# Attention beside two dense layers: sums of a on TensorE, maxima of phi in three steps, later loads, four x buffers, v_m w_in over four turns

## The chip, the cores and the metric

The kernel runs on one core of a Trainium2 chip. The metric is device time in microseconds, from the first to the last work of one launch. The engines are TensorE (PE: matmuls, with its weight loads listed apart as PEld), VectorE (DVE), ScalarE (ACT), GpSimd (POOL) and SyncE (SP). Each works through its own instructions in program order, and in this kernel SP issues every DMA transfer.

## The reference

```python
# q, k, v: 8 batches x 8 heads x 576 x 64; phi: 8 x 8 x 576 x 32
a = phi - np.max(phi, axis=2, keepdims=True)          # over the 576 positions
a = np.exp(a)
a = a / (np.sum(a, axis=2, keepdims=True) + 1e-09)
k_m = np.einsum('bhsm,bhsd->bhmd', a, k)
v_m = np.einsum('bhsm,bhsd->bhmd', a, v)
scores = np.matmul(q, k_m.transpose(0, 1, 3, 2)) / np.sqrt(64)
attn = softmax(scores)                                 # over the 32 memories
x = np.matmul(attn, v_m)                               # to 4608 tokens x 512
h = x @ moe_w_in;  x = (h - np.tanh(h)) @ moe_w_out    # 512 -> 2048 -> 512
h = x @ moe2_w_in; g = np.where(h > 0, h, np.exp(np.minimum(h, 0)) - 1)
return g @ moe2_w_out
```

## The kernel before, in words

The program has three parts that overlap.

**Attention units.** A unit is one batch and four heads; there are 16 (u = 0 to 15). `Attention.unit` is a generator: each `yield` ends a step, and the program calls every live unit once in a round. A step emits instructions into the engines' queues, so the round in which something is emitted sets its place in the order of every engine. A unit takes, in this order: the maximum of phi over six chunks (L120, DVE), its maximum over partitions by a transpose and a matmul (L125 to L134), the subtraction (L135), the exponential into a (L140, ACT), the sum of a over six chunks (L143, DVE), the matmuls of a with k and v into km (L150) and the sums' column of km (L153), 1/sum (rs), rm, kk and vbd (L159 to L165), transposes of q (L174), scores (L195), the softmax over memories (L199 to L211) and the probabilities split in two parts, phl (L215, L216), stored in DRAM (L222). Units 0 and 2 run in one set of tiles, all others in another; units 0 and 1 do their elementwise work on DVE, the rest on POOL. Tiles of phi and of kv have one buffer, so the load for the next unit must wait until this unit's last reader is done. Units 4 and up start seven rounds apart, so up to three are alive.

**First layer, 64 blocks.** A block is 288 tokens by 512 of the 2048 hidden columns, in two turns (i = 0, 1). Attention is not multiplied out: v_m times w_in is formed first (`vw_half`, L316 to L321: six matmuls, two copies on ACT, two subtractions on DVE for both parities), and a block multiplies the probabilities p with it (`h_unit`, L331). `g_a` to `g_d` compute h - tanh(h): four ACT instructions (L342 to L345; the third writes s), then POOL (L350) and DVE (L351, L356, L357), and a split of s into g by ACT and POOL (L363, L364). `x_unit` multiplies an earlier block's g with w_out (L376) and copies the result to an x tile (L383 on ACT, L385 on DVE), which is stored in DRAM (L391). There are three x tiles, three s tiles, and three PSUM banks (`misc`) that the x matmuls, v_m w_in and the attention units share. A group is four blocks (j = 0 to 3) that share v_m w_in; in the last of them each turn computes two halves of it for the next group. The order of a turn is written out by hand: h_unit, g_a, g_b, an x_unit, a round of conversions of weights, a round of the units, g_d, half of v_m w_in, an x_unit, g_c, a round of the units, the other half.

**Second layer.** From about 945 us on PE multiplies the sums of x with the second pair of weights; its loads (`load_x`, L405) begin in the last blocks of the first layer.

## Time and profile before

| | |
|---|---|
| median of 3 runs | 1772.01 us (1768.45 to 1779.19) |
| the profiled execution | 1771.73 us |
| its span, first to last instruction | 1770.0 us |
| PE / DVE / ACT / POOL busy | 1618.5 / 1225.3 / 954.7 / 766.3 us |
| mean granted TensorE clock | 0.968 |

The profile is of one execution. Busy times are those in which an engine had an instruction running; a wait is the idle time of an engine ahead of an instruction, put down to what ended it. PEclk is the granted share of TensorE's full clock. "SPq" is the queue of SP, whose instructions issue transfers; its waits are times in which nothing behind them can be issued.

### The profile page before, as it was taken

The numbers are of one execution on the slowest core, as the hardware profiler recorded it, in microseconds if no ns is written. First come the engines' busy times: TensorE is split into PE (matmuls) and PEld (weight loads), VectorE is DVE, ScalarE is ACT, GpSimd is POOL, SyncE is SP. The second block draws the span as 40 slices with busy tenths as digits, with TensorE's granted clock in tenths as the row PEclk, the third lists the DMA queues.
The fourth block names the chain that finished last, engine by engine and source line by source line (L and its number), as shares of the span: only waits on it lengthen the run. The fifth ranks groups of instructions, "written<-read, shape, count | busy, mean of one in ns | idle before, by whom it ended". The sixth has DMA issues, their size and how long they took to land.

```text
span 1770.0 us, 30078 instructions
## 1 busy us (share of the span) xinstructions
PE 1618.5 (91%) x11496; PEld 1494.5 (84%) x11496; DVE 1225.3 (69%) x1805; ACT 954.7 (54%) x1713; POOL 766.3 (43%) x539
## 2 busy tenths in 40 slices
PE   4546887987998999999989999999999999999998
PEld 3446777877898999999989999999999999999997
DVE  5768876778899988888854555555555555555554
ACT  2445675766888888888864333333333333333332
POOL 2144554636676666666653222222222222222222
PEclk9668999999999999999999999999999999999999
DMA  9546557567566455666567521212222121111110
GB/s 226 157 121 181 146 158 201 169 191 221 187 225 195 160 177 212 217 215 223 189 191 291 195 61 60 60 60 60 60 60 59 54 58 56 57 60 57 58 36 25
DMA packets 140935, 238.40 MB, mean 135 GB/s; under 512 B 8184, under 2 KB 102392, under 8 KB 138744
## 3 DMA queue, kind: packets, MB, share of 16 engines
q1 hardware_dynamic: 140792, 236.49, 43.0%
q8 instruction: 91, 1.49, 0.4%
q14 instruction: 52, 0.43, 0.1%
HBM read 159.78 MB, written 75.50 MB: 133 GB/s over the span
## 4 chain that ended last, share of the span: by engine, by line
PE 70%; DMA 10%; DVE 7%; ACT 5%; issue 3%; POOL 2%; SPq 1%; DVEq 0%; POOLq 0%; ACTq 0%
PE h_ps L432 23%; PE o_ps L469 22%; PE x_ps L376 14%; PE h_ps L331 8%; DMA x_dram<-x 5%; DMA raw<-in_moe_w_in_dram 3%; PE vw_ps L316 2%; DVE s L356 1%; DVE vw L321 1%; DMA kv<-in_v_dram 1%; ACT t L342 1%; DMA xr<-x_dram 1%; DMA phi<-in_phi_dram 1%; ACT u L343 1%; ACT big L345 1%
## 5 line engine op out<-in xcount | busy, mean ns | idle before, releaser
L376 PE MATMUL x_ps<-g,w 128*128 128x288 f32 x3072 | 454.5, 301 | 30.4 <-DVE vw L321 9.6
L376 PEld LDWEIGHTS x_ps<-g,w 128*128 128x128 f32 x3072 | 427.2, 192 | 41.6 <-ACT x L383 11.0
L458 POOL TENSOR_TENSOR e<-hm,e 128x512 fp32r<-128x512 f32 x144 | 186.8, 1297 | 588.1 <-ACT e L457 435.4
L432 PEld LDWEIGHTS h_ps<-x,wi 128*128 128x128 f32 x3456 | 429.7, 190 | 11.7
L432 PE MATMUL h_ps<-x,wi 128*128 128x256 f32 x3456 | 433.2, 281 | 0.0
L469 PE MATMUL o_ps<-wo,e 128*128 128x512 f32 x1728 | 423.8, 394 | 0.7 <-POOL e L458 0.7
L469 PEld LDWEIGHTS o_ps<-wo,e 128*128 128x128 f32 x1728 | 314.8, 188 | 65.0 <-POOL e L458 1.1
L443 ACT ACTIVATE t_ps<-hm 128x512 f32<-128x512 f32 x144 | 86.7, 602 | 515.1 <-DVE hm L442 515.1
L350 POOL TENSOR_TENSOR v<-t,u 128x576 f32<-128x576 f32 x128 | 183.9, 1436 | 230.8 <-ACT u L343 208.4
L331 PE MATMUL h_ps<-p,vw 128*128 128x288 f32 x1536 | 241.8, 309 | 17.8 <-DVE s L357 6.1
L331 PEld LDWEIGHTS h_ps<-p,vw 128*128 128x128 f32 x1536 | 222.9, 199 | 20.9 <-issue 12.7
L364 POOL TENSOR_TENSOR g<-s,g 128x576 fp32r<-128x576 f32 x128 | 203.2, 1588 | 83.9 <-ACT g L363 81.3
L449 DVE SCALAR_TENSOR_TENSOR hm<-hm,t_ps 128x512 f32<-128x512 f32 x144 | 99.1, 688 | 200.6 <-ACT hm L444 200.6
L442 DVE TENSOR_SCALAR hm<-h_ps 128x512 f32<-128x512 f32 x144 | 99.6, 692 | 139.9 <-PE h_ps L432 139.9
L351 DVE TENSOR_TENSOR h_ps<-h_ps,t 128x576 f32<-128x576 f32 x128 | 97.9, 765 | 56.8 <-ACT u L343 55.6
L342 ACT ACTIVATE t<-h_ps 128x576 f32<-128x576 f32 x128 | 83.2, 650 | 82.2 <-PE h_ps L331 39.6
L356 DVE SCALAR_TENSOR_TENSOR s<-s,v 128x576 f32<-128x576 f32 x128 | 121.5, 949 | 1.8 <-POOL v L350 1.8
L321 DVE TENSOR_TENSOR vw<-vw_ps,vw 64x512 fp32r<-64x512 f32 x128 | 88.1, 688 | 40.4 <-ACT vw L319 38.4
L357 DVE COPY_PREDICATED s<-big,h_ps 128x576 f32<-128x576 uint32 x128 | 106.3, 831 | 11.3 <-DVE s L356 0.5
L345 ACT ACTIVATE big<-u,bias 128x576 f32<-128x576 f32 x128 | 97.5, 762 | 13.5 <-DVE s L357 13.5
L451 DVE TENSOR_TENSOR hm<-hm,h_ps 128x512 f32<-128x512 f32 x144 | 98.9, 687 | 5.0
L450 DVE SCALAR_TENSOR_TENSOR hm<-hm,t_ps 128x512 f32<-128x512 f32 x144 | 98.9, 687 | 4.9
(86 smaller groups left out, 1764.6 us busy)
## 6 DMA issues: line engine op xcount, KB each, us to landing
x_dram<-x SPq DMA_DIRECT2D x128, 288.0 KB
xr<-x_dram SPq DMA_DIRECT2D x72, 512.0 KB
p<-p_dram SPq DMA_DIRECT2D x62, 576.0 KB
raw<-in_moe_w_in_dram SPq DMA_DIRECT2D x32, 512.0 KB
raw<-in_moe_w_out_dram SPq DMA_DIRECT2D x32, 512.0 KB
w_dram<-wst SPq DMA_DIRECT2D x32, 512.0 KB
kv<-in_k_dram SPq DMA_DIRECT2D x16, 576.0 KB
kv<-in_v_dram SPq DMA_DIRECT2D x16, 576.0 KB
```

The costliest lines, as they stand in the source:

```text
L321: nc.vector.tensor_tensor(lo, src, r32(hi), op=ALU.subtract)
L331: nc.tensor.matmul(ps[:, j, :NB], lhsT=vw[a][:, kc, 128 * j:128 * j + 128], rhs=p[:, kc, b, :], start=(k == 0), stop=(k == 5))
L342: nc.scalar.activation(t, w[0], ACTF.Tanh)
L345: nc.scalar.activation(big, u, ACTF.Relu, bias=bias[:, 1:2])
L350: nc.gpsimd.tensor_tensor(v, t, u, op=ALU.mult)
L356: nc.vector.scalar_tensor_tensor(s, s, G_B, v, op0=ALU.add, op1=ALU.mult)
L357: nc.vector.copy_predicated(s, big.bitcast(U32), d)
L364: nc.gpsimd.tensor_tensor(g[:, 1], s, r32(g[:, 0]), op=ALU.subtract)
L376: nc.tensor.matmul(ps, lhsT=wo[pg][:, a, j, 128 * dm:128 * dm + 128], rhs=g[:, b, j, :], start=(k == 0), stop=(k == 11))
L432: nc.tensor.matmul(ps[:, j], lhsT=w3[:, a, kc, 128 * j:128 * j + 128], rhs=x[:, b, kc, :], start=(k == 0), stop=(k == 11))
L458: nc.gpsimd.tensor_tensor(e[:, 1], hm, r32(e[:, 0]), op=ALU.subtract)
L469: nc.tensor.matmul(self.acc[n][tg], lhsT=e[:, a, j, 128 * tg:128 * tg + 128], rhs=w4[:, b, j, :], start=(pg == 0 and j == 0 and i == 0), s ...
```

## The change

- The sum of a over chunks on DVE (L143) and its tile go, and so does the round that it had. In place of four matmuls of the sums with ones there are six, one for each chunk, with a (128 columns) as weights.
- The maximum of phi is taken in three two-input steps (384, 128 and 128 elements) in place of one reduction. The first uses the buffer of pT.
- vbd is made by two instructions with two scalars each; rm goes.
- The load of phi for units 2 and up is issued by ACT. The loads of kv and q come after a `yield`, so a round behind the instructions that free their tiles. For units 4 and up a `yield` is put ahead of the store of phl.
- x has four buffers, s (`gw`) two.
- From block 26 on the halves of v_m w_in for the next group are computed in the four turns of j = 2 and 3, one in each. A second pool holds the tiles of the odd parity for every other group.

```diff
@@ -82,8 +82,7 @@
         self.kv = fix.tile([128, 2, 4, 6, D], F32, name="kv")
         self.a = fix.tile([128, 6, 4, M], F32, name="a")
         self.kT = fix.tile([128, 4, 2, M], F32, name="kT")
-        self.asum = fix.tile([128, 4, M], F32, name="asum")
-        for t in (self.a, self.asum, self.kv):
+        for t in (self.a, self.kv):
             nc.gpsimd.memset(t[96:], 0.0)
         nc.gpsimd.memset(self.kT, 0.0)
 
@@ -99,7 +98,7 @@
             nc.sync.dma_start(out=t[:96, 1], in_=view("v", 0, 4))
         elif what == "phi":
             t = self.wk.tile([96, 4, 6, M], F32, tag="phi", name="phi")
-            nc.sync.dma_start(out=t, in_=view("phi", 0, 4))
+            (nc.sync if u < 2 else nc.scalar).dma_start(out=t, in_=view("phi", 0, 4))
         else:
             t = self.q_p.tile([96, 2, 6, D], F32, tag="q", name="q")
             nc.sync.dma_start(out=t, in_=view("q", 0 if what == "q0" else 2, 2))
@@ -111,13 +110,16 @@
         b, g = divmod(u, 2)
         par = b % 2
         ident = self.ident
-        kv, a, kT, asum = self.kv, self.a, self.kT, self.asum
+        kv, a, kT = self.kv, self.a, self.kT
         ps_tile = lambda shape, name: self.ps.tile(shape, F32, tag="m", name=name)
 
         ph = self.loaded.pop((u, "phi"))
         row = lambda name: wk.tile([128, 4, M], F32, tag="cmax", name=name)
         cmax = row("cmax")[:96]
-        nc.vector.tensor_reduce(cmax, ph.rearrange("p h c m -> p h m c"), axis=AX.X, op=ALU.max)
+        top = wk.tile([128, S], F32, tag="pT", name="top")[:96, :12 * M].rearrange("p (h c m) -> p h c m", h=4, c=3)
+        nc.vector.tensor_tensor(top, ph[:, :, 0:3], ph[:, :, 3:6], op=ALU.max)
+        nc.vector.tensor_tensor(cmax, top[:, :, 0], top[:, :, 1], op=ALU.max)
+        nc.vector.tensor_tensor(cmax, cmax, top[:, :, 2], op=ALU.max)
         yield
         if u >= 4:
             yield
@@ -140,8 +142,6 @@
         nc.scalar.activation(a[:96].rearrange("p c h m -> p h c m"), ph, ACTF.Exp)
         self.load(nxt, "phi")
         yield
-        nc.vector.tensor_reduce(asum[:96], a[:96].rearrange("p c h m -> p h m c"), axis=AX.X, op=ALU.add)
-        yield
         self.loaded.pop((u, "kv"))
         km = ps_tile([128, 2 * D + 2], "km")
         kmv = km[:, :2 * D].rearrange("p (t d) -> p t d", t=2)
@@ -149,21 +149,20 @@
             for h in range(4):
                 nc.tensor.matmul(kmv[32 * h:32 * h + 32], lhsT=a[:, c, h, :], rhs=kv[:, :, h, c, :],
                                  start=(c == 0), stop=(c == 5))
-        for h in range(4):
-            nc.tensor.matmul(km[32 * h:32 * h + 32, 2 * D:], lhsT=asum[:, h], rhs=self.ones[:, :2],
-                             start=True, stop=True)
-        self.load(nxt, "kv")
+        for c in range(6):
+            nc.tensor.matmul(km[:, 2 * D:], lhsT=a[:, c].rearrange("p h m -> p (h m)"), rhs=self.ones[:, :2],
+                             start=(c == 0), stop=(c == 5))
         rs = sm.tile([128, 1], F32, tag="rs", name="rs")
-        rm = sm.tile([128, 2, 1], F32, tag="rm", name="rm")
         twice = lambda t: kmv[:, t].rearrange("p (o d) -> p o d", o=1).to_broadcast([128, 2, D])
         nc.vector.tensor_scalar(rs, km[:, 2 * D:2 * D + 1], GUARD, None, op0=ALU.add)
         nc.vector.reciprocal(rs, rs)
-        nc.vector.tensor_scalar(rm[:, :, 0], self.pmask, rs, None, op0=ALU.mult)
         kk = wk.tile([128, 2, D], F32, tag="kk", name="kk")
         nc.vector.tensor_scalar(kk, twice(0), rs, None, op0=ALU.mult)
         vbd = wk.tile([128, 2, D], F32, tag="vbd", name="vbd")
-        nc.vector.tensor_tensor(vbd, twice(1), rm.to_broadcast([128, 2, D]), op=ALU.mult)
-        yield
+        for j in range(2):
+            nc.vector.tensor_scalar(vbd[:, j], kmv[:, 1], rs, self.pmask[:, j:j + 1], op0=ALU.mult, op1=ALU.mult)
+        yield
+        self.load(nxt, "kv")
         s = self.sc_p.tile([128, 18, M], F32, tag="s", name="s")
         for pr in range(2):
             qt = self.loaded.pop((u, f"q{pr}"))
@@ -174,9 +173,9 @@
                     nc.tensor.transpose(pq[:, c2, :], qt[:, h, 2 * c2:2 * c2 + 2, :].rearrange("p c d -> p (c d)"),
                                         ident[:96, :96])
                 nc.scalar.activation(qT[:, h], pq, ACTF.Copy)
+                yield
                 if h == 1:
                     self.load(nxt, f"q{pr}")
-                yield
             if pr == 0:
                 kT_ps = ps_tile([128, 2, 128], "kT_ps")
                 nc.tensor.transpose(kT_ps[:, 0, :], kk.rearrange("p h d -> p (h d)"), ident)
@@ -215,6 +214,8 @@
         nc.scalar.activation(phl[:, :, 0], pTv, ACTF.Copy)
         eng.tensor_tensor(phl[:, :, 1], pTv, r32(phl[:, :, 0]), op=ALU.subtract)
         yield
+        if u >= 4:
+            yield
         for c, t in enumerate(first_p or ()):
             for hq in range(2):
                 r0 = 64 * hq + 32 * c
@@ -287,11 +288,12 @@
         self.tc, self.nc, self.const = tc, tc.nc, const
         self.p_dram, self.x2_dram = p_dram, x2_dram
         pool = lambda name, n, **kw: ctx.enter_context(tc.tile_pool(name=name, bufs=n, reuse_waits="tile", **kw))
-        self.x_p = pool("x2", 3)
+        self.x_p = pool("x2", 4)
         self.g_p = pool("g", 4)
-        self.gw, self.gw1 = pool("gw", 3), pool("gw1", 1)
+        self.gw, self.gw1 = pool("gw", 2), pool("gw1", 1)
         self.p_p = pool("p", 3)
         self.vw_p = pool("vw", 1)
+        self.vw2_p = None
         self.vw, self.p, self.g, self.x2, self.work, self.x2_pool = {}, {}, {}, {}, {}, {}
 
     def new_p(self, sw, n):
@@ -307,7 +309,8 @@
         nc = self.nc
         if po == 0:
             for par in pars:
-                self.vw[par, pg] = [self.vw_p.tile([128, 2, 256], F32R, tag=f"vw{pg % 2}_{par}{t}", name="vw")
+                pool = self.vw2_p if self.vw2_p and par and pg // 2 % 2 else self.vw_p
+                self.vw[par, pg] = [pool.tile([128, 2, 256], F32R, tag=f"vw{pg % 2}_{par}{t}", name="vw")
                                     for t in range(2)]
         ps = self.misc.tile([128, 2, 256], F32, tag="m", name="vw_ps")
         for kc in range(2):
@@ -698,8 +701,12 @@
                 while nss == 0 and not all(u in p_done for u in range(2 * (nxt[1] // 2) + 2)):
                     units.round()
 
-            vw_next = None
-            if bi == 1:
+            vw_next = vw_spread = None
+            if j >= 2 and bi >= 26:
+                if bi // 4 + 1 < len(groups):
+                    nss, nbp, nsub = groups[bi // 4 + 1]
+                    vw_spread = (nbp, 2 * (2 * nss + nsub) + j - 2)
+            elif bi == 1:
                 vw_next = (0, 0, (1,))
             elif j == 3 and nxt:
                 vw_next = (nbp, 2 * nxt[0], (0, 1))
@@ -712,7 +719,9 @@
             if at1_open and 2 * B - 1 in p_done:
                 at1_ctx.close()
                 at1_open = False
-                wt_p[3], wt_p[2] = new(l1c, "wt3", 1), new(late_ctx, "wt2", 1)
+                wt_p[3] = new(l1c, "wt3", 1)
+                m1.vw2_p = new(l1c, "vw2", 1)
+                wt_p[2] = new(late_ctx, "wt2", 1)
                 cv.first.extend(conv_l1("o", 4, 5))
             if bi == 14:
                 cv.todo.extend(conv_l2)
@@ -760,6 +769,10 @@
                 units.round()
                 if vw_next:
                     m1.vw_half(vm[vbp], wi[vpg + i], vpg + i, 1, pars)
+                if vw_spread:
+                    vbp, vpg = vw_spread
+                    need("i", vpg)
+                    m1.vw_half(vm[vbp], wi[vpg], vpg, i)
                 pend.append((n, pg))
             if ss == 0 and sub == 0 and j == 1:
                 save_vm(bp)
```

## Rows read from the trace of the kernel before

**Rows 1.** Windows by stage: length, busy us (instructions), clock, DMA share, GB/s
```profile
0.00:80.00 80.00, 38.70 (x343) 27.31 (x344) 54.34 (x105) 25.01 (x55) 18.84 (x22) 0.87 0.87 208
80.00:480.00 400.00, 317.91 (x2651) 286.92 (x2650) 303.66 (x465) 263.56 (x517) 206.06 (x141) 0.91 0.58 171
480.00:895.00 415.00, 398.83 (x2962) 394.17 (x2962) 373.35 (x553) 355.56 (x618) 285.69 (x197) 0.99 0.58 200
895.00:945.00 50.00, 43.05 (x294) 42.64 (x293) 28.22 (x39) 29.30 (x49) 26.58 (x17) 0.90 0.82 244
945.00:1770.00 825.00, 820.01 (x5254) 743.50 (x5252) 465.78 (x646) 281.26 (x475) 229.12 (x163) 1.00 0.22 71
```

**Rows 2.** Waits of SP's queue, 80 to 480 us: us in total, times, longest
```profile
SPq L102 <- ACT a L140: 100.0, 9, 13.3
SPq L391 <- ACT x L383: 36.6, 11, 7.6
SPq L222 <- POOL phl L216: 32.2, 6, 21.4
SPq L98 <- PE km L153: 31.8, 9, 6.6
```

**Rows 3.** Waits of all engines, 80 to 480 us
```profile
ACT x L383 <- DMA x_dram<-x: 30.1, 10, 5.8
...
PE vw_ps L316 <- ACT x L383: 15.6, 9, 4.2
...
PE h_ps L331 <- DMA p<-p_dram: 6.0, 2, 3.8
```

**Rows 4.** Groups by line, 80 to 480 us: busy us, mean ns | idle before
```profile
L120 DVE TENSOR_REDUCE cmax<-phi 96x128 f32<-96x768 f32 x12 | 18.5, 1545 | 0.0
L143 DVE TENSOR_REDUCE asum<-a 96x128 f32<-96x768 f32 x12 | 18.5, 1541 | 3.6 <-ACT a L140 3.6
...
L201 DVE TENSOR_TENSOR s<-s,smax 128x576 f32<-128x576 f32 x14 | 15.3, 1096 | 0.5
L161 DVE TENSOR_SCALAR rm<-pmask,rs 128x2 f32<-128x2 f32 x12 | 8.4, 699 | 0.4
...
L165 DVE TENSOR_TENSOR vbd<-km,rm 128x128 f32<-128x128 f32 x12 | 3.3, 278 | 0.0
...
L153 PE MATMUL km<-ones,asum 128*32 128x2 f32 x96 | 2.8, 172 | 0.0
```

**Rows 5.** Line L201, all 16: least/median/most ns, first and last start
```profile
L201 DVE TENSOR_TENSOR s<-s,smax x16: 757/759/1877, 46.1 to 477.3; 128x576 f32<-128x576 f32 x16
```

**Rows 6.** Timeline around one unit's km: start us, us, instruction
```profile
346.70 0.84 ACT L140 ACTIVATE a<-phi 96x768 f32<-96x768 f32 x1
...
349.01 1.83 PE L376 MATMUL x_ps<-g,w 128*128 128x288 f32 x12
...
351.44 1.52 PE L150 MATMUL km<-kv,a 128*32 128x128 f32 x48
```

**Rows 7.** Lines L102 and L391, the issue on SP: least/median/most ns
```profile
L102 SPq DMA_DIRECT2D phi<-in_phi_dram x16: 312/330/459, 0.7 to 408.2; - x16
...
L391 SPq DMA_DIRECT2D x_dram<-x x128: 354/363/3586, 143.0 to 960.6; - x128
```

**Rows 8.** Groups by line, 0 to 80 us, DVE
```profile
L120 DVE TENSOR_REDUCE cmax<-phi 96x128 f32<-96x768 f32 x4 | 6.4, 1589 | 6.1 <-DMA phi<-in_phi_dram 6.1
L143 DVE TENSOR_REDUCE asum<-a 96x128 f32<-96x768 f32 x4 | 5.8, 1454 | 0.0
```

**Rows 9.** One of the windows of 20 us between 480 and 895 us
```profile
660.00:680.00 20.00, 19.04 (x145) 18.66 (x144) 16.89 (x26) 17.73 (x32) 14.01 (x10) 1.00 0.60 212
```

**Rows 10.** Timeline of a steady block: L364 and the L344 two turns later
```profile
819.20 1.79 POOL L364 TENSOR_TENSOR g<-s,g 128x576 fp32r<-128x576 f32 x1 [1.42 <-ACT g L363]
...
820.58 0.78 ACT L344 ACTIVATE s<-u,bias 128x576 f32<-128x576 f32 x1
```

**Rows 11.** Waits, 895 to 945 us
```profile
DVE x L385 <- DMA x_dram<-x: 8.1, 2, 7.5
```

## Prediction

> **What bounds the kernel now.** I read the windows first, to see in which stretch TensorE (PE) is not the bound. PE is busy unevenly: in the last stage 820 of 825 us, from 480 to 895 us 398.8 of 415, from 895 to 945 us 43.1 of 50, but from 80 to 480 us, where attention runs beside the first 22 blocks, 317.9 of 400, and 38.7 of 80 ahead of that [rows 1]. The change touches nothing in the last stage, so all that it can give lies in four stretches: 82 us of idle PE in the second, 16 in the third, 7 in the fourth, and the start, which is a chain of transfers and VectorE (DVE) work.
>
> Then the waits of the SP queue from 80 to 480 us. SP issues every transfer in program order, and it stood 100 us waiting for the Exp of L140 so that it could load the next phi, 32 us for phl, 32 us for the matmuls of km [rows 2]. Each time it stands, the stores of x that come behind it stand too. The third view, all waits of the same stretch, shows what that does: ScalarE (ACT) sat 30.1 us, ten times, until a store of x had freed one of three buffers, and PE sat 15.6 us at vw_ps until ACT's copy of x had come, and 6.0 us for p, also loaded by SP [rows 3]. So the stretch is set by one in-order queue handing its delay to another. DVE, busy 304 of 400 us, is the next limit there.
>
> **The parts, 80 to 480 us.** It holds 12 units (4 to 15).
>
> *Queue and x buffers.* The phi load goes to ACT's queue, right behind the Exp that it waits for; the kv and q loads are emitted a round behind the matmuls that free their tiles, the store of p a round behind phl. SP's waits of 100, 32 and 32 us lose their reason. The fourth x buffer gives each store one tile's time more: two tiles in a block, 22 blocks in 400 us, so 9 us, over the longest of the ten waits, 5.8 us. I take the 30.1 us of ACT as gone. PE feels only part: it saw 15.6 us at vw_ps, and some of those waits are for an ACT that is merely busy. From 0 to 30 us; I take 15. For p, of the 6.0 us, I take 4.
>
> *DVE.* Per unit the sum over a goes (1.54 us), and rm (0.70 us on average for 128x2 elements) [rows 4]. vbd becomes two instructions of 64 columns in place of one of 128 at 0.28 us: between 0 and 0.28 us more, I take 0.2. The maximum (1.55 us) becomes three steps of two inputs. Such an instruction over 576 took 0.76 us at the median [rows 5], one over 128 took 0.28; on the line between them 384 takes 0.55, and with two of 128 that is 1.11 us, 0.43 less. But the one over 576 averaged 1.10 us in this stretch [rows 4] and once took 1.88: the excess over the quiet price is 0.34 us on the mean. Paid three times it makes 2.1 us, 0.6 more. I take 0.1 more. The sum: -1.54 - 0.70 + 0.2 + 0.1 = -1.94 us per unit, -23 us for twelve. DVE is busy three quarters of the time and on the path in part of it: 0 to 23 us, I take 10.
>
> What the Trainium skill says of this term speaks against the three steps. "SBUF — State Buffer", section "Who interferes with whom", states that a VectorE instruction with two SBUF inputs contends with GpSimd's reads, while tensor_reduce on trn2 never contends. The 1.88 us against a median of 0.76 agree with the first half. By the page alone the three steps would cost their 0.6 us more each unit, 7 us of DVE in all, some 3 us of the forecast; without it they would give 5 us of DVE, some 2 us.
>
> *PE.* Eight matmul records of 32 columns at 0.17 us apiece, overlapped [rows 4], become twelve with 128 columns of weights. The x matmuls, 128 columns of weights and 288 moving, took 1.83 us for 12 [rows 6]; that bounds the new ones from above, the 48 records of km in 1.52 us (0.38 for 12) from below. I take 1.1 against 0.3, so 0.8 us a unit, 10 us for twelve, of which I charge 6 as PE is the bound four fifths of the time.
>
> *Order.* Without the sum's own round everything from km on comes a round earlier, and km waits for the Exp directly. In the unit shown the Exp began at 346.70 and took 0.84 us; one round ahead of km at 351.44 PE stands at the x matmuls of 349.01 [rows 6]. There 1.5 us are to spare, but ACT is often later than here: 0 to 2 us a unit on a PE behind which the h and x matmuls queue; I take 3 in all. For units 0 to 3 the store of p comes a round earlier, for the others in the same round as before.
>
> *ACT.* It now issues the phi loads. On SP such an issue took 0.31 to 0.46 us [rows 7]; behind it on ACT are tanh, the squares and the copies of x, for which PE waits. Eleven of the fourteen fall in this stretch, 3.6 us at 0.33; ACT is busy two thirds of the time, so I charge 2. The other end is the store of x, up to 3.59 us in the same queue: 39 us.
>
> Sum of the stretch: -15 - 4 - 10 + 6 + 3 + 2 = -18 us.
>
> **0 to 80 us.** Four units' sums cost DVE 5.8 us here, 1.45 each, and the maximum waits 6.1 us for phi [rows 8]. Three steps are cheaper while POOL is nearly idle (18.8 of 80 us busy). From 0 to 9 us; I take 5, and nothing for the wait on phi: the transfer is issued at the same point and only on another queue. The Trainium skill, "DMA: Bandwidth & Descriptors", section "Issuing engines are not separate DMA queues", says that DMAs of all engines run on the same 16 engines and a second issuer saves only sequencer time. By it the 6.1 us stay; no row of before can show it, for there every load is SP's.
>
> **480 to 895 us.** Every other window of 20 us has PE at 19.04 or a little over, as the one shown does [rows 9]: once in four blocks, at j == 3, two turns carry two halves of v_m w_in each, and DVE and ACT fall behind. After the change the four turns of j == 2 and 3 carry one half each, nine times from block 26 on. 9 x 0.96 is 8.6; I take 8 of the 16 us (0 to 14). The price is the s buffer, three to two: s of a turn (L344) must wait until g of two turns ago (L364) is done. In a steady block L344 begins at 820.58, L364 ended at 819.20 + 1.79 = 820.99 [rows 10], so ACT would be 0.4 us late. If that came in two turns of eight it is 0.1 us a turn over 76 turns, 8 us of ACT; ACT is idle 59 of the 415 us and can hide it. From 0 to 8; I take 2. The v_m load of a group is now read about a block sooner after its issue; no row shows a wait for it, so 0 to 5.8 us (the longest wait for a transfer above) for four loads; I take 0.
>
> **895 to 945 us.** Loads of the last stage hold up the stores, and DVE waits 8.1 us for an x buffer [rows 11]. A fourth buffer adds about 5 us of room (two tiles in a block of 10.9 us, 415 us for 38 blocks). Of 7 us of idle PE I take 3.
>
> **Sum.** -18 - 5 - 8 + 2 - 3 = -32 us. The profiled execution took 1771.7 us around its span of 1770.0, the median of the runs is 1772.0, so the sum stands for the runs as well: 1740 us, 1.8% less.
>
> **The rivals.** *The stalls move* (1762 us). PE's wait for x turns into a wait for ACT or DVE that is late anyway, only half of the 15 + 4 + 10 us comes (14), and the costs of 11 us eat most of it: -3, and -7, half of what I take, from the other stretches. For it: PE waited for DVE's and POOL's results too in that stretch. Against it: the ten waits for the store are whole idle time on an engine that has work queued.
>
> *More comes loose* (1710 us). The granted clock averaged 0.91 from 80 to 480 us [rows 1]. If half of the 82 us of idle goes (41), and 317.9 us of PE at a mean clock raised to 0.95 lose 4% where it is the bound (13, of which I take 7), then -48 - 5 - 8 + 2 - 3 = -62. For it: SP's waits held up loads of weights and p as well as x. Against it: DVE and ACT are busy 304 and 264 of 400 us, so they soon bind.
>
> *ACT stands at the issue* (1794 us, slower). If a phi load on ACT's queue takes as long as SP's worst stores do when the transfers back up, and the wait for Exp's end is added, ACT loses 4 us at each of 14 loads: 56, less the 34 that the rest gives without the 2 us charged for it, is +22. It decides against the change from 2.4 us an issue on (34 / 14). For it: x stores took up to 3.59 us, and until now SP's long waits emptied the queue just ahead of each phi load. Against it: all 16 phi loads took under 0.5 us.
>
> *It does not do what it says*: if SP just stands at the next wait (phl of units 2 and 3, where it stood 21.4 us, keeps its place), that is the first rival's result.
>
> **How the numbers follow.** Forecast 1740 (1725 to 1755): 0.50. Stalls move: 0.20. More comes loose: 0.20. ACT stands at the issue: 0.10. The range reaches from within the third case to the end of the second, 1702 to 1772, which leaves out the slower case and a tail of the good one. About 1% (18 us) is what a measurement of this kernel can tell from no change. Under 1754: nearly all of the forecast's case and all of the third, 0.70; within 1%: 0.21; slower: 0.09.
>
> **What the next profile would show.** SP's wait for L140 gone from 80 to 480 us, ACT's wait for the store of x under 5 us, and PE's idle time there down from 82 to about 60 us: the queue's part. The phi issue on ACT near 0.33 us: the price. cmax near 1.6 us in sum over three steps, with single steps over 1 us beside POOL. PE at 19.7 or more in every 20 us window from 600 to 895: the spread. An L344 that waits for L364 more than 0.2 us a turn would show the lost s buffer, and PE waiting for Exp at km the lost round. I am wrong if PE's idle time stays above 75 us, for then another engine set that stretch.

## The result and the profile after

The changed kernel takes 1757.19 us, the median of 5 runs (1754.31 to 1763.56); beside it the kernel before took 1773.53 (1768.45 to 1779.19). The ratio is 0.9908, with a 95% interval of 0.9879 to 0.9937: 16 us faster, half of the 32 that were forecast. The profiled execution took 1757.19 us around a span of 1755.2.

The change renumbers the lines. The maximum is now L120 to L122, Exp L142, the column sums on PE L153, the load of phi L101, vw L319 to L324, g of a block L345 to L367, the copy of x L386 and its store L394.

The windows of the changed kernel, in the stages of [rows 1] (the first five numbers behind the length are PE, PEld, DVE, ACT and POOL):

```profile
0.00:80.00 80.00, 51.81 (x386) 37.33 (x386) 53.46 (x115) 29.04 (x63) 21.21 (x22) 0.70 0.89 212
80.00:480.00 400.00, 323.05 (x2686) 292.79 (x2686) 285.44 (x479) 261.58 (x514) 206.40 (x141) 0.91 0.57 172
480.00:895.00 415.00, 405.78 (x3048) 402.89 (x3047) 375.61 (x557) 364.21 (x632) 296.72 (x201) 1.00 0.60 206
```

From 480 to 895 us PE is idle for 9 us where it was 16. From 80 to 480 us it is idle for 77 us where it was 82, although DVE was relieved of 18 us (303.66 to 285.44). So the third stage did what was forecast, and the second hardly moved. SP's queue there, to be read against [rows 2] (us in total, times, longest):

```profile
SPq L394 <- ACT x L386: 107.2, 22, 9.4
SPq L223 <- POOL phl L215: 65.1, 12, 22.6
SPq L97 <- PE km L150: 25.3, 8, 6.4
SPq L104 <- PE pq L173: 24.2, 9, 5.4
```

The 100 us that SP stood for Exp are gone, and SP now stands 107 us for ACT's copies of x, where it stood 37: it is ahead of its work, as it should be. Its waits for phl and for km, which the later loads were to take away, are 65.1 and 25.3 us where they were 32.2 and 31.8. All waits of the same stretch, against [rows 3]:

```profile
PE mT L127 <- DVE cmax L122: 21.1, 6, 11.6
...
DVE rs L157 <- PE km L153: 14.3, 10, 3.4
...
PE x_ps L379 <- ACT x L386: 11.5, 11, 2.4
DVE top L120 <- DMA phi<-in_phi_dram: 11.3, 2, 6.1
...
ACT cv_m L48 <- DMA raw<-in_moe_w_in_dram: 10.9, 1, 10.9
...
PE vw_ps L319 <- ACT x L386: 5.9, 8, 1.3
```

ACT's 30.1 us for the store of x have no row left, and PE's wait at vw_ps for ACT's copy fell from 15.6 us to 5.9, while that at x_ps rose from 4.8 to 11.5. Two more waits have grown: PE for cmax, 7.2 us before, and DVE at rs for the matmuls of km, 2.5 us before. Of the waits for loads, DVE's for phi is new; ACT's for raw weights (the int64 blocks that cv converts) was there before, 12.3 us in three.

Fixed windows mix the start with what follows, so the table below cuts each profiled execution at the starts of first-layer blocks (L342 of before, L345 of after). It is worked out from the trace; us, in brackets PE's idle time. The start itself varies by some 4 us between executions of the same code, and a profiled execution can lie up to 10 us from its kernel's median, so the medians and ratios decide and the table says where.

```
kernel        to block 0   0-1    2-21          28-59   median    ratio  [95% interval]
before            80.3    50.9   347.6 (58.3)   343.3   1773.5    1
after             71.4    62.3   342.6 (45.9)   334.6   1757.2    0.9908 [0.9879, 0.9937]
one part of the change on the kernel before
e1_spread         75.8    48.3   358.3 (66.9)   337.9   1773.4    0.9980 [0.9967, 0.9993]
e13_s2            76.2    50.3   353.8 (66.4)   346.0   1779.0    1.0014 [0.9991, 1.0036]
e2_x4s2           77.1    48.1   342.6 (55.8)   345.9   1761.9    0.9918 [0.9903, 0.9933]
e3_loads          75.9    46.9   342.0 (53.0)   344.0   1766.4    0.9949 [0.9932, 0.9966]
e4_sums           72.7    63.1   340.7 (39.7)   345.3   1767.3    0.9953 [0.9932, 0.9975]
e14_sums_cv6      75.8    47.1   343.0 (46.5)   344.2   1765.0    0.9934 [0.9909, 0.9958]
one part of the changed kernel undone or mended
e7_phisp          70.3    63.5   334.4 (38.6)   334.6   1748.7    0.9847 [0.9815, 0.9878]
e12_phi_late      74.0    61.9   339.1 (44.7)   334.6   1757.2    0.9905 [0.9888, 0.9921]
e8_reduce         71.6    63.2   337.7 (43.1)   335.6   1755.6    0.9890 [0.9852, 0.9929]
e5_cv6            75.5    49.4   348.7 (47.8)   335.3   1751.6    0.9854 [0.9824, 0.9884]
e6_round4         75.9    53.7   337.3 (42.7)   336.4   1755.8    0.9877 [0.9847, 0.9907]
e9_sp_cv          74.9    45.2   335.4 (39.7)   335.2   1743.9    0.9815 [0.9792, 0.9837]
e10_sp_cv_red     74.9    47.5   334.1 (35.3)   334.6   1740.3    0.9806 [0.9785, 0.9827]
e11_sp_cv_x3s3    76.2    49.3   350.7 (50.1)   340.4   1768.3    0.9960 [0.9940, 0.9980]
```

From before to after: the start gives 8.9 us, blocks 0 and 1 take 11.4 back, blocks 2 to 21 give 5.0, blocks 22 to 27 2.1, blocks 28 to 59 8.7, and all that follows 1.4. That is the difference of the two spans, 14.8 us, but for rounding. Up to block 22 it is 2.4 us, where the forecast had 23; behind it 12.4, where it had 9. What has to be explained is the 11.4 and why 2 to 21 gave so little. Part of the 8.9 is chance: e1_spread, e13_s2 and e2_x4s2 run the code of before up to block 0 and reached it at 75.8 to 77.1 us.

The chain of waits shows a candidate for each. From 134 to 476 us (start, us, what) its longest pieces hold two loads of phi:

```profile
271.55 18.91 DMA p<-p_dram
290.54 13.08 DMA phi<-in_phi_dram
324.42 13.29 DMA phi<-in_phi_dram
```

The piece of p is a transfer counted from its issue; the longest wait that ended with it is ACT's, 2.5 us. Around blocks 0 and 1 the chain holds one load of raw weights, here in the timeline (start, us, instruction; in square brackets the idle time before it and what ended it):

```profile
107.51 0.89 SPq L533 DMA_DIRECT2D raw<-in_moe_w_in_dram  x2
...
122.09 0.62 ACT L48 ACTIVATE cv_m<-raw 128x512 f32<-128x512 f32 x1 [10.87 <-DMA raw<-in_moe_w_in_dram]
...
123.10 1.22 PE L319 MATMUL vw_ps<-w,vm 128*128 128x256 f32 x4 [7.96 <-ACT qT L175]
...
123.69 0.69 DVE L324 TENSOR_TENSOR vw<-vw_ps,vw 64x512 fp32r<-64x512 f32 x1 [12.45 <-ACT vw L322]
```

ACT stands 10.87 us at a conversion whose raw block was issued at 107.51 us. Behind it in ACT's order are qT and vw, and so PE and DVE stand too. The kernel before waits for its block as well, but later, at the end of block 1:

```profile
128.81 0.64 ACT L48 ACTIVATE cv_m<-raw 128x512 f32<-128x512 f32 x1 [8.24 <-DMA raw<-in_moe_w_in_dram]
```

There PE's longest wait for ACT from 80 to 131 us was 2.5 us. So it is the place of this conversion that differs, more than the wait itself.

### The profile page after: what moved, and what is told of

It is laid out like the page before. It is cut to its first block, busy times and chain, and to the rows that moved or that the text cites. A ratio compares the mean times of both kernels' runs of the same rounds, so it can differ in the third digit from the quotient of the medians.

```text
span 1755.2 us, 30367 instructions
## 1 busy us (share of the span) xinstructions
PE 1629.3 (93%) x11560; PEld 1504.8 (86%) x11560; DVE 1199.4 (68%) x1821; ACT 954.8 (54%) x1713; POOL 771.3 (44%) x537
## 4 chain that ended last, share of the span: by engine, by line
PE 73%; DVE 8%; DMA 7%; ACT 6%; issue 3%; POOL 1%; SPq 0%; ACTq 0%; DVEq 0%; POOLq 0%
PE h_ps L435 23%; PE o_ps L472 23%; PE x_ps L379 15%; PE h_ps L334 8%; PE vw_ps L319 2%; DMA p<-p_dram 2%; DMA raw<-in_moe_w_in_dram 2%; DMA phi<-in_phi_dram 2%; ACT t L345 1%; DVE vw L324 1%; PE km L150 1%; DVE h_ps L354 1%; ACT u L346 1%; ACT big L348 1%; DVE cv_m L54 1%
## 5 line engine op out<-in xcount | busy, mean ns | idle before, releaser
L379 PE MATMUL x_ps<-g,w 128*128 128x288 f32 x3072 | 443.8, 298 | 18.4 <-ACT x L386 11.5
L379 PEld LDWEIGHTS x_ps<-g,w 128*128 128x128 f32 x3072 | 420.7, 190 | 23.5 <-ACT x L386 13.6
L367 POOL TENSOR_TENSOR g<-s,g 128x576 fp32r<-128x576 f32 x128 | 205.1, 1602 | 90.7 <-ACT g L366 89.2
L452 DVE SCALAR_TENSOR_TENSOR hm<-hm,t_ps 128x512 f32<-128x512 f32 x144 | 99.0, 688 | 200.5 <-ACT hm L447 200.5
L354 DVE TENSOR_TENSOR h_ps<-h_ps,t 128x576 f32<-128x576 f32 x128 | 97.9, 765 | 66.7 <-ACT u L346 61.4
L345 ACT ACTIVATE t<-h_ps 128x576 f32<-128x576 f32 x128 | 83.3, 651 | 78.5 <-PE h_ps L334 36.3
L359 DVE SCALAR_TENSOR_TENSOR s<-s,v 128x576 f32<-128x576 f32 x128 | 115.1, 899 | 5.0 <-POOL v L353 2.7
L324 DVE TENSOR_TENSOR vw<-vw_ps,vw 64x512 fp32r<-64x512 f32 x128 | 87.8, 686 | 37.5 <-ACT vw L322 35.4
L347 ACT ACTIVATE s<-u,bias 128x576 f32<-128x576 f32 x128 | 99.6, 778 | 16.2 <-POOL g L367 5.6
```

What stands on the lines that cost most here:

```text
L324: nc.vector.tensor_tensor(lo, src, r32(hi), op=ALU.subtract)
L354: nc.vector.tensor_tensor(h, h, t, op=ALU.subtract)
L359: nc.vector.scalar_tensor_tensor(s, s, G_B, v, op0=ALU.add, op1=ALU.mult)
L367: nc.gpsimd.tensor_tensor(g[:, 1], s, r32(g[:, 0]), op=ALU.subtract)
L379: nc.tensor.matmul(ps, lhsT=wo[pg][:, a, j, 128 * dm:128 * dm + 128], rhs=g[:, b, j, :], start=(k == 0), stop=(k == 11))
```

## The experiments

The theory is that the parts give what was forecast and that two things take half of it back: phi, which lands late once SP runs ahead, and the conversions of weights, of which one round falls behind the start of block 0. Its rivals are that the parts gave less to begin with, that the three maxima lose the time on DVE beside POOL, and that the third s buffer was worth more than was charged.

**One part at a time, on the kernel before.** These ask which parts give what, and whether their gains add.

*The spread of v_m w_in, with two s buffers* (x stays at three, all else as before):

```diff
-        self.gw, self.gw1 = pool("gw", 3), pool("gw1", 1)
+        self.gw, self.gw1 = pool("gw", 2), pool("gw1", 1)
...
+            if j >= 2 and bi >= 26:
...
+                    vw_spread = (nbp, 2 * (2 * nss + nsub) + j - 2)
...
+                if vw_spread:
...
+                    m1.vw_half(vm[vbp], wi[vpg], vpg, i)
```

> The kernel before with the four-turn spread of v_m w_in alone (its second pool, and s with two buffers, which make its room). Theory A (each part is worth what it shows by itself, and the third stretch is TensorE-bound once the spread is in): 9 group ends at 0.96 us, so -8 to -10 us, all of it from block 26 on, and nothing ahead of it. Theory B (the two s buffers cost as much as the spread gives): -3 us or less, with L344 waiting for L364.

Measured: 0.998, 3.5 us, between the two theories. Blocks 28 to 59 went from 343.3 to 337.9 us; from 480 to 895 us ACT waited 12.7 us for POOL's g, of which the kernel before has no row. PE's idle time in blocks 2 to 21, which the spread does not reach, was higher, at 66.9. That may be the buffer that it gives up, as the next run suggests.

*Two s buffers in place of three, alone*:

```diff
-        self.gw, self.gw1 = pool("gw", 3), pool("gw1", 1)
+        self.gw, self.gw1 = pool("gw", 2), pool("gw1", 1)
```

> The kernel before with two s buffers in place of three, nothing else. Theory A (the lost s buffer costs what the forecast charged, 0 to 8 us, 2 taken): 1 to 4 us above before. Theory B (it costs much more where attention runs, as blocks 2 to 21 were 11 us longer in the run with the spread alone): 8 to 14 us above before, most of it in blocks 2 to 21, with L344 waiting for GpSimd.

Measured: 1.0014 (0.9991 to 1.0036), 2.5 us at the middle and not to be told from nothing. The forecast had charged 2. ACT's wait for POOL's g is 11.3 us here.

*Four x buffers and two of s*:

```diff
-        self.x_p = pool("x2", 3)
+        self.x_p = pool("x2", 4)
...
-        self.gw, self.gw1 = pool("gw", 3), pool("gw1", 1)
+        self.gw, self.gw1 = pool("gw", 2), pool("gw1", 1)
```

> The kernel before with four x buffers and two s buffers alone. Theory A (the store of x bounds blocks 2 to 21): ScalarE's 30.1 us of waiting for a store fall under 5 us and the time falls by 10 to 15 us. Theory B (the wait only covers an engine order that is late anyway): the 30 us go, the time falls by 5 us or less, and TensorE waits as long for copies of x that come late for another reason.

Measured: 0.9918, 14.5 us, and ACT's wait for the store of x is 0 where it was 30.1. The fourth buffer alone gives nearly as much as the whole change.

*The loads alone* (phi on ACT's queue, kv and q a round later):

```diff
-            nc.sync.dma_start(out=t, in_=view("phi", 0, 4))
+            (nc.sync if u < 2 else nc.scalar).dma_start(out=t, in_=view("phi", 0, 4))
...
-        self.load(nxt, "kv")
...
         yield
+        self.load(nxt, "kv")
...
+                yield
                 if h == 1:
                     self.load(nxt, f"q{pr}")
-                yield
```

> The kernel before with phi for units 2 and up loaded by ScalarE and the loads of kv and q a round later; x keeps three buffers, the sums stay on VectorE. Theory A (SP's 100 us of waiting for Exp hold up the stores): with the stores free three buffers suffice, ScalarE's wait for a store falls from 30 to under 10 us, and -8 to -15 us. Theory B (a phi transfer that SP used to issue into an empty queue now lands behind others): VectorE waits 5 to 15 us for phi, and the time is within 5 us of before.

Measured: 0.9949, 9 us, the time of theory A without its reason: ACT's wait for the store fell only to 16.3 us, and a wait of DVE for phi appeared, 2.8 us, that the kernel before did not have after 80 us.

*The sums on TensorE alone*:

```diff
-        nc.vector.tensor_reduce(asum[:96], a[:96].rearrange("p c h m -> p h m c"), axis=AX.X, op=ALU.add)
-        yield
...
-        for h in range(4):
-            nc.tensor.matmul(km[32 * h:32 * h + 32, 2 * D:], lhsT=asum[:, h], rhs=self.ones[:, :2],
-                             start=True, stop=True)
+        for c in range(6):
+            nc.tensor.matmul(km[:, 2 * D:], lhsT=a[:, c].rearrange("p h m -> p (h m)"), rhs=self.ones[:, :2],
+                             start=(c == 0), stop=(c == 5))
...
         yield
+        if u >= 4:
+            yield
```

> The kernel before with the sums of a on TensorE alone (six matmuls with a as weights, the sum's round gone, a round ahead of the store of phl instead). Theory A (VectorE is on the path in four tenths of the time): 1.54 us of VectorE less in each of 16 units, TensorE 0.8 us more, so -4 to -8 us. Theory B (the six matmuls cost about as much TensorE time as the sum did on VectorE): within 3 us, with TensorE's busy time up 10 us or more.

Measured: 0.9953, 8.4 us. The start falls to 72.7 and blocks 0 and 1 rise to 63.1: this part alone brings the whole give-back of the changed kernel at that place.

The four gains (3.5, 14.5, 9 and 8.4) add to 35 us, near the forecast's 32, and together they made 16. So the parts work, and something is lost where they meet. Part of it is that the fourth x buffer and the loads take away the same wait: of ACT's 30.1 us the one removes all and the other 13.8. The loss in blocks 0 and 1 is not of this kind, since it lies within the 8.4 already.

**Who loses it: phi.** *The load of phi back on SP's queue, all else changed*:

```diff
-            (nc.sync if u < 2 else nc.scalar).dma_start(out=t, in_=view("phi", 0, 4))
+            nc.sync.dma_start(out=t, in_=view("phi", 0, 4))
```

> The changed kernel with all loads of phi back on SP's queue, at the same place in the program. Theory A (SP's wait for Exp holds up the stores): SP stands about 100 us for Exp again, ScalarE waits for x stores under 10 us thanks to the fourth buffer, and the time rises by 5 to 10 us. Theory B (with four x buffers SP's standing costs nothing, and phi lands sooner in an empty queue): VectorE's wait for phi after 80 us, 11.3 us, falls to zero, and the time falls by up to 8 us.

Measured: 0.9847, with an interval (0.9815 to 0.9878) that lies just below that of the changed kernel. Blocks 2 to 21 fell from 342.6 to 334.4 us and DVE's wait for phi is gone. SP's queue, 80 to 480 us:

```profile
SPq L101 <- ACT a L142: 95.1, 10, 12.9
SPq L394 <- ACT x L386: 50.9, 14, 6.2
SPq L223 <- POOL phl L215: 29.6, 4, 22.6
```

SP stands 95 us for Exp once more, and the kernel is faster for it. With four x buffers its wait does not reach ACT: no wait for a store of x is left in this stretch.

The two slow loads of the changed kernel fall in blocks 11 and 13. Those two blocks, in us, from the same cut of the traces (all kernels with four x buffers; the last three load phi on SP right behind Exp):

```
kernel          block 11   block 13
after               23.1       20.2
e8_reduce           22.4       19.8
e5_cv6              22.1       19.7
e6_round4           21.7       19.6
e7_phisp            18.6       13.3
e9_sp_cv            18.6       13.4
e10_sp_cv_red       18.6       13.4
```

So the late phi costs 11.4 us in these two blocks; e7_phisp loses 3 of them again in others.

*Phi on SP, but a round later*:

```diff
-            (nc.sync if u < 2 else nc.scalar).dma_start(out=t, in_=view("phi", 0, 4))
+            nc.sync.dma_start(out=t, in_=view("phi", 0, 4))
...
+        yield
         self.load(nxt, "phi")
-        yield
```

> The changed kernel with phi loaded by SP a round behind the Exp, so that SP no longer stands for Exp and its queue is not emptied ahead of the load. Theory A (phi lands late on ScalarE's queue since other transfers are in flight): from issue to the last packet 5 to 13 us here too, VectorE waits 10 us or more for phi, and the time is 5 to 10 us above that of the run with phi on SP right behind the Exp. Theory B (ScalarE's queue is slow by itself): phi lands within 3 to 4 us on SP, VectorE waits under 5 us, and the time is as with phi on SP.

Measured: 0.9905, the changed kernel's time, and a wait like the changed kernel's, but longer (all waits, 80 to 480 us):

```profile
DVE top L120 <- DMA phi<-in_phi_dram: 21.7, 2, 12.2
```

So it is not ACT's queue as such, as theory A has it. One of the two waits falls in block 1, which was no longer than in the changed kernel, the other in block 11, which took 26.9 us; block 13 took 13.3. Of units 5 to 15, the packets of the trace give the time from the issue of phi to its last packet: 3.0 us on average in the kernel before (2.4 to 4.9), 5.6 in the changed one (2.7 to 12.8), 3.7 with phi on SP, 6.4 with it on SP and late (two at 14.7 or more). In the kernel before at most 1.0 MB of other transfers moved meanwhile; beside the two slow loads of the changed kernel, 12.0 and 12.8 us, it was 2.5 and 2.3 MB.

*One reduction in place of the three maxima*, the rival by which DVE lost the time beside POOL:

```diff
-        top = wk.tile([128, S], F32, tag="pT", name="top")[:96, :12 * M].rearrange("p (h c m) -> p h c m", h=4, c=3)
-        nc.vector.tensor_tensor(top, ph[:, :, 0:3], ph[:, :, 3:6], op=ALU.max)
-        nc.vector.tensor_tensor(cmax, top[:, :, 0], top[:, :, 1], op=ALU.max)
-        nc.vector.tensor_tensor(cmax, cmax, top[:, :, 2], op=ALU.max)
+        nc.vector.tensor_reduce(cmax, ph.rearrange("p h c m -> p h m c"), axis=AX.X, op=ALU.max)
```

> The changed kernel with the maximum of phi taken by one reduction again. Theory A (three steps cost as much as one reduction, since the two-input steps collide with GpSimd): within 3 us either way, VectorE's busy time within 5 us. Theory B (they save 0.4 us each as where GpSimd is quiet): VectorE's busy time up by 7 us, the time up by 3 to 6 us.

Measured: 0.9890 against 0.9908, 1.6 us, well inside both intervals. The rival falls as the cause of the missing half.

**Who loses it: the conversion round.** The loop that runs the first units also converts weights ahead of block 0, one round of cv for each round of units from the seventh on:

```
        while 1 not in p_done:
            units.round()
            if units.rounds >= 7:
                cv.round()
```

Without the sum's round, unit 1 is done a round sooner: 13 rounds of conversions lie ahead of block 0 in place of 14. By the code, the last block of w_out that was loaded at the start is then not converted when the x matmuls of block 1 ask for it; their `need` adds a round of conversions within that turn, and so the next block of w_in is converted in the turn in which its load was issued, not one turn later. That is the raw block for which ACT stood 10.87 us. *One round of conversions sooner, on the changed kernel*:

```diff
-            if units.rounds >= 7:
+            if units.rounds >= 6:
```

> The changed kernel with the rounds of weight conversion ahead of block 0 started one round sooner, so that as many of them lie there as in the kernel before. Theory A (without the sum's round the prologue has one conversion round less, and the two conversions that are short then stop ScalarE in block 1): blocks 0 and 1 fall from 62 to about 50 us and the time to about 1746. Theory B (it is the order of the four first units' own steps against the blocks that costs): blocks 0 and 1 stay at 60 us or more, the time within 3 us of the changed kernel.

Measured: 0.9854 (0.9824 to 0.9884, which just touches the changed kernel's interval). Blocks 0 and 1 fell from 62.3 to 49.4 us; the start is 4 us longer. The median, 1751.6 us, lies between the theories.

*The same on the kernel with the sums alone*, so that none of the loads is in play:

```diff
-            if units.rounds >= 7:
+            if units.rounds >= 6:
```

> The run with the sums on TensorE alone, and the conversions' rounds one round sooner. Theory A (the 12 us that blocks 0 and 1 lose belong to the sums' lost round by way of the conversions): blocks 0 and 1 fall from 63 to about 50 us, and the time to 6 to 10 us under that of the sums alone. Theory B (they belong to the order of the four first units' steps): blocks 0 and 1 stay above 58 us.

Measured: blocks 0 and 1 fell from 63.1 to 47.1 us, below the 50.9 of before. The total moved by 2 us only (0.9934 against 0.9953, intervals that overlap): the place is shown, its worth in this kernel is not.

*The round given back to units 0 to 3*:

```diff
         yield
+        if u < 4:
+            yield
         self.loaded.pop((u, "kv"))
```

> The changed kernel with an empty round in the place of the sums' round for units 0 to 3 alone, so that their steps stand against the conversions and the blocks as before. Theory A and B both have blocks 0 and 1 back at about 50 us, the start 2 to 4 us later, and a gain of 5 to 10 us over the changed kernel; if this run gains and the one with the earlier conversions does not, it was the order of the steps. Theory C (the 11 us that blocks 0 and 1 lose are VectorE work that was merely put off from the start): no gain, blocks 0 and 1 at 60 us.

Measured: blocks 0 and 1 at 53.7 us, the start back at 75.9; 0.9877, not to be told from the changed kernel's 0.9908, so the gain of 5 to 10 us is not shown. Block 1 took 20.5 us, block 0 33.2.

Over all traces the place is plain. With 13 rounds ahead of block 0 (the changed kernel, e4, e7, e8, e12) block 1 took 31.1 to 32.8 us and block 2 began at 133.7 to 135.9; with 14 (all others) it took 19.4 to 24.7 and block 2 began at 120.1 to 131.2.

**Both mended.** *Phi on SP and the conversions a round sooner* (the edits of e7_phisp and e5_cv6):

```diff
-            (nc.sync if u < 2 else nc.scalar).dma_start(out=t, in_=view("phi", 0, 4))
+            nc.sync.dma_start(out=t, in_=view("phi", 0, 4))
...
-            if units.rounds >= 7:
+            if units.rounds >= 6:
```

> The changed kernel with both repairs: phi loaded by SP, and the conversions' rounds one round sooner. Theory A (the two give-backs are separate: 8 us from blocks 2 to 21 for phi, 9 us from the start for the conversions): 1738 to 1743 us, 2 per cent under the kernel before, with blocks 0 and 1 near 50 us and blocks 2 to 21 near 335. Theory B (each repair only uncovers the other stretch's limit): 1748 us or more.

Measured: 1743.9 us, 0.9815, 31 us below the kernel before (1775.1 beside it) and just above the range of theory A, with blocks 0 and 1 at 45.2 and blocks 2 to 21 at 335.4 us. The window of the profiled execution, which at 1735.3 us is the fastest of the five:

```profile
80.00:480.00 400.00, 337.80 (x2827) 308.02 (x2826) 309.16 (x506) 277.51 (x542) 218.49 (x151) 0.94 0.62 185
```

PE is now idle for 62 us from 80 to 480, where the forecast had said about 60.

*The same with one reduction for the maximum* (the edits of e9_sp_cv and e8_reduce):

```diff
-        nc.vector.tensor_tensor(top, ph[:, :, 0:3], ph[:, :, 3:6], op=ALU.max)
...
+        nc.vector.tensor_reduce(cmax, ph.rearrange("p h c m -> p h m c"), axis=AX.X, op=ALU.max)
```

> The run with both repairs, and the maximum of phi by one reduction as well. Theory A (three steps cost 0.45 us of VectorE more per unit beside GpSimd, 7 us in all, a third of it on the path): 1 to 4 us under the run with both repairs. Theory B (they are off the path): within 1 us of it, and VectorE's busy time 7 us lower.

Measured: 1740.3 us, 0.9806, the lowest of all; against e9_sp_cv the intervals overlap nearly whole, so three steps or one makes no difference that these runs can tell.

*The same as e9_sp_cv with three x and three s buffers*:

```diff
-        self.x_p = pool("x2", 4)
+        self.x_p = pool("x2", 3)
...
-        self.gw, self.gw1 = pool("gw", 2), pool("gw1", 1)
+        self.gw, self.gw1 = pool("gw", 3), pool("gw1", 1)
```

> The run with both repairs with three x and three s buffers in place of four and two. Theory A (the fourth x buffer is what frees ScalarE, SP still stands about 95 us for Exp): ScalarE waits 10 to 20 us for x stores again and the time is 8 to 15 us longer than with four. Theory B (the third s buffer is worth as much as the fourth x buffer once the loads of kv and q come later): within 4 us, the wait for x stores under 10 us, and no wait of s for GpSimd.

Measured: 1768.3 us, 24 us more than e9_sp_cv and more than either theory, and ACT's wait for the store is back (all waits, 80 to 480 us):

```profile
ACT x L386 <- DMA x_dram<-x: 24.2, 8, 3.8
```

This is the change's largest part: with phi on SP, it is the fourth buffer that bears SP's waits.

## Why the prediction was wrong

The direction was right and the time lies in the range, but half of the gain was given back at two places that the working had at nothing or nearly so. That the time is in the range says little: the range takes in the first rival, whose time it nearly is. Up to block 22 almost nothing came of the 23 us (2.4), and behind it a little more than was forecast.

**Where it failed first: "Queue and x buffers" has no term for a phi that lands late; the one reason given stands in the part on the start: "nothing for the wait on phi: the transfer is issued at the same point and only on another queue."** In the first 80 us, of which this was said, the wait did not grow: 6.1 us became 1.8. From 80 to 480 us it came. The issue was priced, and rightly: 0.33 us forecast, and on ACT's queue it took this (least, median and most ns, first and last start):

```profile
L101 ACTq DMA_DIRECT2D phi<-in_phi_dram x14: 319/320/386, 11.7 to 411.3; - x14
```

The landing was not priced. Standing for Exp, SP had kept its other transfers back, so that phi went out with little else in flight. Once ACT issues phi, SP runs ahead, and its loads and stores are in flight. One of the two slow loads, and the DVE instruction that takes it:

```profile
290.54 0.32 ACTq L101 DMA_DIRECT2D phi<-in_phi_dram  x1
...
303.64 0.56 DVE L120 TENSOR_TENSOR top<-phi 96x384 f32<-96x384 f32 x1 [6.13 <-DMA phi<-in_phi_dram]
304.23 0.29 DVE L121 TENSOR_TENSOR cmax<-top 96x128 f32<-96x128 f32 x1
304.55 0.29 DVE L122 TENSOR_TENSOR cmax<-cmax,top 96x128 f32<-96x128 f32 x1
304.76 0.76 DVE L354 TENSOR_TENSOR h_ps<-h_ps,t 128x576 f32<-128x576 f32 x1
```

DVE stands 6.1 us at the maximum of a later unit, and the block's own L354 is queued behind it. PE stands too: its waits for cmax are 9.6 us in blocks 2 to 21, where the kernel before has none and e7_phisp 3.1. And PE then runs at half its clock, the level of 1.2 GHz, for a while. From 302 to 306 us it had been busy for 0.7 of 4 us. The window behind that, with the granted clock third from the end, first in the changed kernel and then in e7_phisp:

```profile
306.00:312.00 6.00, 5.05 (x22) 5.08 (x23) 5.82 (x12) 1.65 (x3) 1.16 (x1) 0.50 0.37 133
306.00:312.00 6.00, 5.62 (x40) 4.68 (x39) 5.36 (x11) 5.22 (x10) 4.05 (x3) 1.00 0.48 170
```

The price is the 11.4 us of blocks 11 and 13, or 8 over all of blocks 2 to 21. The forecast had seen the mechanism from the wrong side: it named SP's wait as what emptied the queue just ahead of each phi load, and used that only for the issue on ACT. The Trainium skill, "DMA: Bandwidth & Descriptors", section "Issuing engines are not separate DMA queues", says that DMAs of all engines run on the same 16 and interleave. The trace agrees that a second queue is no separate path: phi took 5.6 us to land on it, where it had taken 3.0. The prediction applied this to the first 80 us alone.

**Where it failed second: "Order" and "0 to 80 us."** The lost round was priced as km waiting for Exp, 3 us. That is small in the trace, 3.4 us of PE's weight loads in the stretch, where it had been 2.7. That a round of units also carries a round of conversions stood in the code of the start loop and was not followed. It put one round behind the start of block 0 and so brought up the conversion in block 1 for which ACT stood 10.87 us, ahead of qT and vw. Blocks 0 and 1 lost 11.4 us; the start gained 8.9 for the 5 forecast, or some 5 against the other executions of that code. e4_sums has the loss with no other part, e5_cv6 and e14_sums_cv6 take it away. What that is worth in the whole kernel is less sure: 5.6 us between the medians in e5_cv6, 1.4 in e6_round4, 4.7 from e7_phisp to e9_sp_cv.

**The other steps.**
- *x buffers*: right for ACT. The 30.1 us went, and e11_sp_cv_x3s3 shows that the wait comes back without them. For PE the 15 us were too much: all its waits in blocks 2 to 21 that ended with ACT's copy of x, summed from the trace, went from 30.1 to 20.0 us. The buffer alone gives 14.5 us and the loads 9, but the two remove the same wait, so they do not add. That SP's waits for phl and km would go was wrong: 65.1 and 25.3 us are left.
- *DVE*: 18.2 us less in the stretch, for 23 forecast. But DVE now stands 14.3 us at rs until the matmuls of km and of the sums are done, where it stood 2.5; the working had no term for it, and no run tells what it costs. The three maxima took the upper bound, 0.775 + 0.648 + 0.738 = 2.16 us a unit against 1.55. The Trainium skill, "SBUF — State Buffer", section "Who interferes with whom", states that a VectorE instruction with two SBUF inputs contends with GpSimd's reads and that tensor_reduce on trn2 does not. The trace agrees: of the 32 instructions of L121 and L122, the 17 beside which POOL had nothing running took 0.29 us each, as above; others took up to 1.55 (least, median and most ns):

```profile
L121 DVE TENSOR_TENSOR cmax<-top x16: 286/289/1552, 4.8 to 420.8; 96x128 f32<-96x128 f32 x16
```

  On the time, e8_reduce and e10_sp_cv_red show no effect that can be told.
- *vbd*: 2 x 0.334 = 0.67 us, 0.39 more than before and above the bound of 0.28.
- *PE*: the sums took 1.5 us a unit for 0.23, so 15 us raw for the 10 forecast. Busy time of PE in blocks 2 to 21 rose by 7, near the 6 charged. The groups by line, 80 to 480 us (busy us, mean ns | idle before):

```profile
L153 PE MATMUL km<-ones,a 128*128 128x2 f32 x144 | 18.0, 253 | 0.0
...
L120 DVE TENSOR_TENSOR top<-phi 96x384 f32<-96x384 f32 x12 | 9.3, 775 | 11.3 <-DMA phi<-in_phi_dram 11.3
L122 DVE TENSOR_TENSOR cmax<-cmax,top 96x128 f32<-96x128 f32 x12 | 8.9, 738 | 0.4
L121 DVE TENSOR_TENSOR cmax<-top 96x128 f32<-96x128 f32 x12 | 7.8, 648 | 0.4
L163 DVE TENSOR_SCALAR vbd<-km,rs,pmask 128x64 f32<-128x64 f32 x24 | 7.0, 334 | 0.0
```

- *Spread*: right, 8.7 us in blocks 28 to 59 for 8, though 5.4 in e1_spread alone. The windows that the forecast counted are those from 600 us on. From 600 to 895 us PE was idle for 6.8 us and now is not at all; the 9 us that are left lie ahead of that. The window of [rows 9] is now full:

```profile
660.00:680.00 20.00, 20.00 (x154) 20.00 (x153) 19.31 (x30) 18.53 (x33) 13.77 (x10) 1.00 0.57 196
```

- *s buffer*: right. ACT's wait for POOL's g from 480 to 895 us, 0.06 us a turn over 76 turns, is small, though with three x buffers it was 11.3 us (e13_s2), and that run puts the whole at 2.5 us or nothing:

```profile
ACT s L347 <- POOL g L367: 4.6, 7, 1.4
```

- *895 us on*: 1.4 us for 3.

**The rivals.** The time is near that of "the stalls move" (1762), and its reason holds in part: PE's waits for ACT's copies fell by 10 us of 30, and 9.6 us of waits for DVE's cmax came up. But these had the causes named above: with both places mended PE's idle time went down to 62 us, its waits for cmax in blocks 2 to 21 to 3.1, and the gain came. "More comes loose" (1710) did not happen, with either kernel. "ACT stands at the issue" did not happen, at 0.39 us for the longest. Its neighbour did, a load that lands late rather than an issue that takes long. The mark that was set for being wrong, PE idle for more than 75 us from 80 to 480, was met with 77.

**What stays open.** How the repairs divide the 16 us by which e9_sp_cv beats the changed kernel: e7_phisp gives some 11 alone and e5_cv6 some 10, which would be more than 16 together, and each ratio is uncertain by 5 us either way. In e5_cv6 blocks 2 to 21 are 6 us longer than in the changed kernel: 3.5 of them are in block 2, which e9_sp_cv and e14_sums_cv6 also have longer, and the rest is open. So is block 0 of e6_round4, long in spite of its 14 rounds. A second buffer for phi, which would part the load from Exp, was not tried.

## What to carry to other kernels

A queue that stands is also a throttle: before a load is moved away from it, ask what the queue will issue in the time it gains, and price the landing of the load beside that traffic, not only its issue. A buffer more at the place that waits can make the queue's own wait harmless, and is the smaller change. When a step or a round is taken out of a hand-made schedule, list all that advances once a round, not only the work of that step.

## What the runs showed of the hardware

- A load of 288 KB in 384 packets landed in 2.4 to 4.9 us beside at most 1.0 MB of other transfers, and in 12.0 and 12.8 us beside 2.5 and 2.3 MB, issued on another queue than those. Issued on the same queue a round late it took up to 14.8.
- PE ran at full clock until a stand of some 4 us, and then at a granted clock of 0.50 (1.2 GHz) from 306 to 312 us; in e7_phisp, without that stand, the granted clock there was 1.00.
- Matmuls with 128x128 weights and two moving columns of f32 took 253 ns a record; the four-way ones of 32 columns had taken 172 [rows 4].
- A DVE instruction of 128 columns with two SBUF inputs took 0.29 us whenever POOL had nothing running, and 0.65 to 0.74 on the mean from 80 to 480 us, where POOL is busy half of the time. The mean is of two kinds: 15 of the 24 there took 0.29 us and nine 1.24 to 1.55.
